# Where the leaves of a streamed weight tree lie in DRAM, and in how many transfers they are sent there

## The chip, the cores and the metric

The kernel runs on one core of one Trainium2 chip. The metric is device time in microseconds (us). Four runs of the kernel before took 1063.92 to 1066.34 us, with a median of 1065.5 us.

## What is computed

The kernel computes an attention block followed by a SwiGLU feed-forward block, all in float32:

```
kv  = einsum('bhsd,bhse->bhde', k, v)              # b 8, h 8, s 576, d 64
out = einsum('bhsd,bhde->bhse', q, kv)
x   = out / sqrt(mean(out*out, -1) + 1e-6) * g_norm  # -> 4608 tokens x 512
g   = x @ w_gate                                   # 512 x 1536
y   = (g * sigmoid(g) * (x @ w_val)) @ w_out       # 1536 x 512
```

## The kernel before

The 4608 tokens are cut into nine blocks of 512. For each block the kernel makes x (attention), then h = silu(x w_gate) * (x w_val) in an "Up" part, then y = h w_out in a "Down" part. The attention work of the next block is laid into these two parts.

**Fewer multiplications by Strassen's scheme.** Block 0 uses plain matrix products. In block 1 the Up part takes one level of a scheme with seven products (numbered 1 to 7) in place of eight. From block 2 on (`DEEP = 2`) the Up part takes two levels, that is 49 products of quarter-size operands; they are executed at L580. Each product needs a linear combination of pieces of w_gate and w_val. Such a combination for outer product o and inner product p is called a leaf (o, p): a [128, 128] tile for each of the two halves f of a pair d. 16 of the 49 leaves lie in the resident weights; the other 33 are made once, in block 1, sent to DRAM, and streamed back in every block from 2 to 8.

**Block 1.** Its Up part has six units, one for each pair j of feature tiles. A unit executes its products in the order 1, 5, then 4 and 3 of the unit before, then 6, 2, 7 (`Up.sequence`). Each product shows as 8 records of TensorE at L431 and takes about 1.73 us. Around them:

- POOL makes three of the operands (t tiles, from a pool of nine buffers) by subtractions at L111, and the products h at L112.
- ACT copies PSUM after product 1 (L447), 6 (L451) and 7 (L482), and takes the SiLU after product 2 (L478) and 4 (L487). All of these accumulate in one PSUM chain b, so product 4 must wait until the copy L482 has read what product 7 left.
- DVE adds (L110) the PSUM chains a and c to tiles r in SBUF, sums parts of h (s and h, `h_sums`), and makes the leaves.

**Making the leaves.** After a product that was the last to use an operand, `multiply` extends a list `making` by the steps of `leaf_steps`: a source is split into quarters, two DVE instructions change one quarter in place, and two more write three further leaves into a room (r for the t tiles, one xi tile for wg and wv, used again by every unit). After each product `make(3)` takes three steps off the list. The last step of each call of `leaf_steps` is `send`, which writes the leaves to DRAM. A pair j thus has 5 + 5 + 5 + 9 = 24 steps.

**Layout in DRAM.** The stream reads leaves in chunks of two, in the order in which the products of blocks 2 to 8 use them (`CHUNKS`, 17 for each d, where d counts two pairs). Before the change every chunk has a DRAM tile of its own, [128, 2, 2, 128] with 2 KB in each partition's row. So a read of a chunk is one contiguous run of 2 KB per partition (L659), and the sends have to pick the leaves of a source apart: two leaves of one source that share a chunk go in one transfer (L711), all others singly (L715). That is 23 transfers for a pair, 138 in all.

**What sets the order.** The instructions of each engine stand in an order that a scheduler makes at build time, by data dependences and program order; the sends among themselves are kept in program order by `tc.keep_in_program_order`. All transfers named here go through the queue of SyncE (SP), which issues them one after the other and waits at each for what it needs: k and v loads (L223), q loads (L238), the sends, the stream loads and the output stores (L814).

**The ring of t tiles.** The nine buffers serve the operands of block 1, then three sets of differences of w_out for the Down part (t<-wo at L111), then the chunks of the stream. A buffer that was sent from is free only when the send has landed.

Of the kernel before, what the change touches and what calls it, by code (L numbers as in the profile page):

```python
# [8 lines left out]
F32 = mybir.dt.float32  # L9
# [5 lines left out]
P = 128  # L15
# [3 lines left out]
def kernel(  # L19
# [41 lines left out]
    nc = tc.nc  # L61
# [11 lines left out]
    NP = NF // 2  # L73
# [5 lines left out]
    def pool(name, bufs, **kw):  # L79
        return ctx.enter_context(tc.tile_pool(name=name, bufs=bufs, **kw))  # L80
# [9 lines left out]
    dram = pool("dram", 1, space=bass.MemoryType.DRAM)  # L90
# [27 lines left out]
    class Words:  # L118
# [12 lines left out]
        def __init__(self, src, shape):  # L131
            self.raw = ld_pool.tile([P, 2 * BLK], U32, name="ld")
            dst = self.raw.rearrange("p (a b) -> p a b", a=shape[0])
            nc.sync.dma_start(out=dst, in_=src)
            self.shape = shape
# [317 lines left out]
    class Up(Quad):  # L453
# [41 lines left out]
        def multiply(self, p):  # L495
            super().multiply(p)
            ffn = self.ffn
            if ffn.n != DEEP - 1:
                return

            if p == 5:
                self.leaf_room = ring().rearrange("p f (s c) -> p (f s) c", c=P)
            if p in (5, 7, 4):
                at = 3 * (5, 7, 4).index(p)
                ffn.making.extend(leaf_steps(self.j, [(self.w[p].unsqueeze(1), (p,))], self.leaf_room[:, at:]))
            if p == 3:
                if ffn.leaf_room is None:
                    ffn.leaf_room = x_pool.tile([P, 3, 7, P], F32, name="xi").rearrange("p a b c -> p (a b) c")
                halves = lambda t: t[self.j].rearrange("p (o i) c -> p o i c", o=2)
                ffn.making.extend(leaf_steps(self.j, [(halves(wg), (1, 2)), (halves(wv), (6, 3))], ffn.leaf_room))  # L510

    class Inner:
# [114 lines left out]
    RESIDENT = (1, 6, 2, 3)  # L627
    QUARTER = {1: (0, 0), 6: (0, 1), 2: (1, 0), 3: (1, 1)}

    CHUNKS = (  # L630
# [5 lines left out]
    class Stream:  # L636


        def __init__(self):
            self.dram = {}  # L640
            for d in range(NP // 2):
                for c in range(len(CHUNKS)):
                    self.dram[d, c] = dram.tile([P, 2, 2, P], F32, name=f"w{d}_{c}")
            self.at = {op: (c, i) for c, ops in enumerate(CHUNKS) for i, op in enumerate(ops)}
            self.tiles, self.uses, self.next, self.held = {}, {}, [], []

        def enable(self, n):
            if DEEP <= n < NB:
                self.next += [(n, d, c) for d in range(NP // 2) for c in range(len(CHUNKS))]
                self.pump()  # L650

        def pump(self):

            while self.next and not self.held[-9]:
                n, d, c = key = self.next.pop(0)
                k = len(CHUNKS[c])
                self.tiles[key] = t_tile(key).rearrange("p l (f c) -> p l f c", f=2)
                self.uses[key] = 2 * k
                nc.sync.dma_start(out=self.tiles[key][:, 0:k], in_=self.dram[d, c][:, 0:k])  # L659

        def use(self, n, d, o, p, f):
            c, i = self.at[o, p]
# [9 lines left out]
    stream = Stream()  # L672

    def t_tile(key=None):

        stream.held.append(key)
        return t_pool.tile([P, 2, 2 * P], F32, name="t")

    def leaf_steps(j, sources, room):


        d, f = divmod(j, 2)
        at = {}
        i = 0
        for t, os in sources:
            n = len(os)
            t = t.rearrange("p o i (e c) -> p o i e c", e=2)
            b11, t2_, b22 = t[:, :, 0, 0], t[:, :, 0, 1], t[:, :, 1, 1]
            to = room[:, i : i + 3 * n].rearrange("p (o r) c -> p o r c", r=3)
            yield lambda b22=b22, t2_=t2_: sub(nc.vector, t2_, b22, t2_)  # L690
            yield lambda b11=b11, t2_=t2_: add(nc.vector, t2_, t2_, b11)
            yield lambda t=t, t2_=t2_, to=to, n=n: sub(
                nc.vector, to[:, :, 0:3:2], t[:, :, 1], t2_.unsqueeze(2).to_broadcast([P, n, 2, P])
            )
            yield lambda b11=b11, t2_=t2_, to=to: sub(nc.vector, to[:, :, 1], b11, t2_)
            for m, o in enumerate(os):
                for r, p in enumerate((4, 7, 5)):
                    at[o, p] = room, i + 3 * m + r
                if o not in RESIDENT:
                    quarters = t[:, m].rearrange("p i e c -> p (i e) c")  # L700
                    for r, p in enumerate((1, 6, 2, 3)):
                        at[o, p] = quarters, r
            i += 3 * n

        def send():
            for c, ops in enumerate(CHUNKS):
                dst = stream.dram[d, c]
                places = [at.get(op) for op in ops]
                if len(ops) == 2 and None not in places and places[0][0] is places[1][0]:
                    (src, i), (_, k) = places  # L710
                    tc.keep_in_program_order(nc.sync.dma_start(out=dst[:, :, f], in_=src[:, i : k + 1 : k - i]))  # L711
                    continue
                for m, place in enumerate(places):
                    if place:
                        tc.keep_in_program_order(nc.sync.dma_start(out=dst[:, m, f], in_=place[0][:, place[1]]))  # L715

        yield send

    class Down(Quad):
        def __init__(self, ffn):  # L720
# [85 lines left out]
    class Ffn:  # L806
# [22 lines left out]
        def up(self, fill):  # L829

            self.s1 = s_pool.tile([P, NP, HB], F32, name="s1")
            units = []
            for d in range(NP // 2):
                if self.n < DEEP:
                    units += [Up(self, 2 * d), Up(self, 2 * d + 1)]
                else:
                    shared = {}
                    units += [Inner(self, d, g, shared) for g in range(4)]
            units[0].prepare()
            last = None  # L840
            for i, this in enumerate(units):
                if i + 1 < len(units):
                    units[i + 1].prepare()
                for unit, p in this.sequence(last):
                    if unit:
                        unit.multiply(p)
                        self.make(3)
                last = this
                fill.get(12 * (i + 1) // len(units), lambda: None)()
            self.down_ = Down(self)  # L850
            self.down_.turn_t(5)
            for unit, p in last.sequence(None):
                if unit is None:
                    last.multiply(p)
# [146 lines left out]
```

## Time and profile before

| | |
|---|---|
| median of 4 runs | 1065.5 us |
| the profiled execution | 1065.41 us, span 1063.6 us |
| PE busy | 1037.6 us, 98% of the span |
| DVE, ACT, POOL busy | 700.7, 245.1, 366.6 us |
| Up part of block 1 | about 162 to 249 us |
| sends to DRAM (w<-t, w<-r, w<-xi) | 138 transfers, 64 or 128 KB each, 1.8 to 2.2 us from issue to landing |
| stream loads (t<-w) | 336 of 256 KB and 21 of 128 KB, median 2.9 and 2.7 us to landing |
| Down part of block 1 | about 249 to 290 us |
| blocks 2 to 6 | about 112 us each |

PE, DVE, ACT, POOL and SP are the engines TensorE, VectorE, ScalarE, GpSimd and SyncE; PEld are TensorE's weight loads. A group "r<-a" is an instruction that writes a tile called r from one called a; L431 is a line of the kernel. In a timeline the columns are start, duration, engine, line, operation, tiles and shapes; a bracket at the end gives the idle time of the engine before it and what ended it. "DMA share" is the mean busy share of 16 DMA engines.

### The profile page before, as it was taken

The numbers are of one execution on the slowest core, as the hardware profiler recorded it, in microseconds if no ns is written. First come the engines' busy times: TensorE is split into PE (matmuls) and PEld (weight loads), VectorE is DVE, ScalarE is ACT, GpSimd is POOL, SyncE is SP. The second block draws the span as 40 slices with busy tenths as digits, with TensorE's granted clock in tenths as the row PEclk, the third lists the DMA queues.
The fourth block names the chain that finished last, engine by engine and source line by source line (L and its number), as shares of the span: only waits on it lengthen the run. The fifth ranks groups of instructions, "written<-read, shape, count | busy, mean of one in ns | idle before, by whom it ended". The sixth has DMA issues, their size and how long they took to land.

```text
span 1063.6 us, 21805 instructions
## 1 busy us (share of the span) xinstructions
PE 1037.6 (98%) x8780; PEld 935.4 (88%) x8780; DVE 700.7 (66%) x1245; ACT 245.1 (23%) x392; POOL 366.6 (34%) x280
## 2 busy tenths in 40 slices
PE   5899999988999999999999999999999999999998
PEld 4644788877899989998999899989999899989997
DVE  2999596778556765576666666666567566765661
ACT  2665111221221211222112211121112221212210
POOL 0000453344025701462156305640456026602670
PEclk8899999998999999999999999999999999999999
DMA  8887103565578326741576246714683265126611
GB/s 236 232 267 224 57 9 107 161 173 160 164 209 251 98 75 193 234 149 61 164 244 170 83 126 229 224 53 129 214 237 77 80 208 190 55 81 189 198 37 40
DMA packets 154644, 161.87 MB, mean 152 GB/s; under 512 B 48432, under 2 KB 105648, under 8 KB 154544
## 3 DMA queue, kind: packets, MB, share of 16 engines
q1 hardware_dynamic: 154480, 160.48, 50.4%
q8 instruction: 70, 1.15, 0.4%
q14 instruction: 30, 0.25, 0.1%
q0 software_dynamic: 64, 0.00, 0.0%
HBM read 138.02 MB, written 22.41 MB: 151 GB/s over the span
## 4 chain that ended last, share of the span: by engine, by line
PE 93%; DVE 3%; SPq 2%; DMA 1%; POOL 1%; issue 0%; ACT 0%; DVEq 0%; POOLq 0%
PE b L580 25%; PE b L431 20%; PE c L580 12%; PE c L431 10%; PE a L580 6%; PE a L431 5%; PE b L882 4%; PE c L882 4%; PE m L255 2%; PE m L339 2%; PE m L292 1%; SPq L223 1%; PE b L292 1%; PE b L272 1%; DMA ld<-in_moe_w_gate_dram 1%; PE m L272 1%
## 5 line engine op out<-in xcount | busy, mean ns | idle before, releaser
L110 POOL TENSOR_TENSOR r<-r 128x256 f32<-128x256 f32 (+1 forms) x105 | 110.2, 1056 | 365.5 <-DVE r L110 361.2
L110 DVE TENSOR_TENSOR r<-b,r 128x512 f32<-128x512 f32 (+1 forms) x273 | 162.3, 607 | 61.3 <-PE b L580 56.5
L110 DVE TENSOR_TENSOR r<-c,r 128x512 f32<-128x512 f32 (+1 forms) x179 | 109.2, 620 | 98.9 <-PE c L580 56.0
L111 POOL TENSOR_TENSOR t<-wo 128x512 f32<-128x512 f32 x81 | 113.2, 1424 | 161.3 <-DVE wo L110 108.5
L580 PE MATMUL b<-x,t 128*128 128x128 f32 x1092 | 151.2, 276 | 0.0
L580 PEld LDWEIGHTS b<-x,t 128*128 128x128 f32 x1092 | 136.0, 192 | 0.6
L110 DVE TENSOR_TENSOR r<-a,r 128x512 f32<-128x512 f32 (+1 forms) x99 | 62.6, 632 | 83.1 <-PE a L580 53.1
L112 POOL TENSOR_TENSOR h<-r 128x1024 f32<-128x1024 f32 (+1 forms) x40 | 81.5, 2053 | 93.2 <-DVE r L110 79.7
L580 PE MATMUL c<-xi,t 128*128 128x128 f32 x840 | 112.1, 275 | 0.0
L580 PEld LDWEIGHTS c<-xi,t 128*128 128x128 f32 x840 | 102.8, 192 | 0.0
L431 PE MATMUL b<-t,h 128*128 128x256 f32 x432 | 97.1, 381 | 0.0
L431 PE MATMUL b<-wo,h 128*128 128x256 f32 x432 | 96.2, 379 | 0.0
L431 PEld LDWEIGHTS b<-wo,h 128*128 128x128 f32 x432 | 81.4, 190 | 10.7
L431 PEld LDWEIGHTS b<-t,h 128*128 128x128 f32 x432 | 80.7, 190 | 11.1 <-issue 0.2
L594 ACT COPY r<-b 128x512 f32<-128x512 f32 x63 | 36.9, 586 | 219.1 <-PE b L580 191.7
L580 PE MATMUL b<-xi,t 128*128 128x128 f32 x588 | 79.7, 276 | 0.0
L580 PEld LDWEIGHTS b<-xi,t 128*128 128x128 f32 x588 | 72.4, 192 | 0.0
L580 PE MATMUL b<-x,wg 128*128 128x128 f32 x336 | 53.0, 280 | 0.0
L580 PE MATMUL b<-x,wv 128*128 128x128 f32 x336 | 51.2, 275 | 0.0
L431 PE MATMUL c<-t,s 128*128 128x256 f32 x216 | 48.9, 383 | 0.0
L431 PE MATMUL a<-wo,h 128*128 128x256 f32 x216 | 48.3, 379 | 0.0
L431 PE MATMUL c<-wo,h 128*128 128x256 f32 x216 | 48.1, 379 | 0.0
(129 smaller groups left out, 1647.2 us busy)
## 6 DMA issues: line engine op xcount, KB each, us to landing
t<-w SPq DMA_DIRECT2D x336, 256.0 KB, 2.9
out_dram<-r SPq DMA_DIRECT2D x17, 512.0 KB, 2.9
ld<-in_q_dram SPq DMA_DIRECT2D x29, 256.0 KB, 4.4
ld<-in_moe_w_gate_dram SPq DMA_DIRECT2D x12, 512.0 KB, 5.1
ld<-in_moe_w_val_dram SPq DMA_DIRECT2D x12, 512.0 KB, 5.2
ld<-in_moe_w_out_dram SPq DMA_DIRECT2D x12, 512.0 KB, 4.3
w<-t SPq DMA_DIRECT2D x36, 128.0 KB, 2.1
ld<-in_k_dram SPq DMA_DIRECT2D x26, 160.0 KB, 3.1
```

Source lines behind the costliest of these rows:

```text
L110: add = lambda e, o, a, b: e.tensor_tensor(out=o, in0=a, in1=b, op=OP.add)
L111: sub = lambda e, o, a, b: e.tensor_tensor(out=o, in0=a, in1=b, op=OP.subtract)
L112: mul = lambda e, o, a, b: e.tensor_tensor(out=o, in0=a, in1=b, op=OP.mult)
L223: nc.sync.dma_start(out=t[r * D : (r + 1) * D, :, 0 : m * D], in_=src[self.n, hs, s0 : s0 + m * D].rearrange("h (p t) d -> p h (t d)", t=m),)
L255: nc.tensor.matmul(self.kv_ps[r][u * D : (u + 1) * D, j, :], lhsT=self.k[j][rows, u, c, :], rhs=self.v[j][rows, u, c, :], start=(c == 0), ...
L272: nc.tensor.transpose(ps[:, j], self.q[t][:, j], ident)
L292: nc.tensor.matmul(self.ps[i][u][p : p + D, t, j, :], lhsT=self.qt[rows, 2 * i + t, j, p : p + D], rhs=kvs[b % 3][rows, j, :], start=True, ...
L339: nc.tensor.transpose(ps[:, e, t], xt[:, t, j + e], ident)
L431: nc.tensor.matmul(banks[e][:, e], lhsT=lhsT, rhs=rhs, start=first and i == 0 and (e == 0 or banks[0] is not banks[1]), stop=i == self.ste ...
L580: nc.tensor.matmul(ps[:, i, f], lhsT=self.weight(o, p, f), rhs=self.operand(o, p), start=first and (i, f) == (0, 0), stop=True, skip_group ...
L594: nc.scalar.copy(out=dst, in_=ps)
L882: nc.tensor.matmul(t, lhsT=w[f // 2][:, i, P * (f % 2) : P * (f % 2 + 1)], rhs=x[:, i, of], start=(i == 0), stop=(i == NS - 1),)
```

## The change

The DRAM tiles of a chunk each give way to one tile for each d, [128, 33, 2, 128], in which the leaves lie in the order in which they are made (`LEAVES`): first the four quarters of each of the sources 5, 7 and 4, then the three further leaves of each source. So four quarters lie side by side, and so do the three (or six) leaves of a room.

`send` now takes one run of leaves. `leaf_steps` yields it as soon as the run is made: for a t source the four quarters after the third step and the three leaves of the room after the fourth; for wg and wv six leaves of xi each. That is 8 transfers for a pair. A pair has 6 + 6 + 6 + 10 = 28 steps, and `up` calls `make(4)` in place of `make(3)`.

A read of a chunk now takes two leaves of the tile with a stride. In 7 of the 17 chunks the two lie side by side (2 KB runs as before), in 9 they don't (two runs of 1 KB), and one chunk has a single leaf.

```
+    LEAVES = [(o, p) for o in (5, 7, 4) for p in (1, 6, 2, 3)]
+    LEAVES += [(o, p) for os in ((5,), (7,), (4,), (1, 2), (6, 3)) for o in os for p in (4, 7, 5)]
...
-            for d in range(NP // 2):
-                for c in range(len(CHUNKS)):
-                    self.dram[d, c] = dram.tile([P, 2, 2, P], F32, name=f"w{d}_{c}")
-            self.at = {op: (c, i) for c, ops in enumerate(CHUNKS) for i, op in enumerate(ops)}
+            self.dram = [dram.tile([P, len(LEAVES), 2, P], F32, name=f"w{d}") for d in range(NP // 2)]
+            self.places = [sorted(map(LEAVES.index, ops)) for ops in CHUNKS]
+            self.at = {LEAVES[i]: (c, m) for c, places in enumerate(self.places) for m, i in enumerate(places)}
...
-                nc.sync.dma_start(out=self.tiles[key][:, 0:k], in_=self.dram[d, c][:, 0:k])
+                nc.sync.dma_start(out=self.tiles[key][:, 0:count], in_=self.dram[d][:, i : k + 1 : max(k - i, 1)])
...
+        def send(leaf, count, src):
+            at = LEAVES.index(leaf)
+            tc.keep_in_program_order(nc.sync.dma_start(out=stream.dram[d][:, at : at + count, f], in_=src))
...
+            if os[0] not in RESIDENT:
+                yield lambda t=t, o=os[0]: send((o, 1), 4, t[:, 0].rearrange("p i e c -> p (i e) c"))
             yield lambda b11=b11, t2_=t2_, to=to: sub(nc.vector, to[:, :, 1], b11, t2_)
-            for m, o in enumerate(os):
-                for r, p in enumerate((4, 7, 5)):
-                    at[o, p] = room, i + 3 * m + r
-                if o not in RESIDENT:
-                    quarters = t[:, m].rearrange("p i e c -> p (i e) c")
-                    for r, p in enumerate((1, 6, 2, 3)):
-                        at[o, p] = quarters, r
+            yield lambda i=i, n=n, o=os[0]: send((o, 4), 3 * n, room[:, i : i + 3 * n])
             i += 3 * n
-
-        def send():
-            for c, ops in enumerate(CHUNKS):
...
-        yield send
...
-                        self.make(3)
+                        self.make(4)
```

More of the change, by code (lines that the diff above doesn't have):

```diff
@@ L639, in __init__ @@
         def __init__(self):
-            self.dram = {}
-            for d in range(NP // 2):
-                for c in range(len(CHUNKS)):
-                    self.dram[d, c] = dram.tile([P, 2, 2, P], F32, name=f"w{d}_{c}")
-            self.at = {op: (c, i) for c, ops in enumerate(CHUNKS) for i, op in enumerate(ops)}
+            self.dram = [dram.tile([P, len(LEAVES), 2, P], F32, name=f"w{d}") for d in range(NP // 2)]
+            self.places = [sorted(map(LEAVES.index, ops)) for ops in CHUNKS]
+            self.at = {LEAVES[i]: (c, m) for c, places in enumerate(self.places) for m, i in enumerate(places)}
             self.tiles, self.uses, self.next, self.held = {}, {}, [], []
@@ L655, in pump @@
                 n, d, c = key = self.next.pop(0)
-                k = len(CHUNKS[c])
+                i, k = self.places[c][0], self.places[c][-1]
+                count = len(CHUNKS[c])
                 self.tiles[key] = t_tile(key).rearrange("p l (f c) -> p l f c", f=2)
-                self.uses[key] = 2 * k
-                nc.sync.dma_start(out=self.tiles[key][:, 0:k], in_=self.dram[d, c][:, 0:k])
+                self.uses[key] = 2 * count
+                nc.sync.dma_start(out=self.tiles[key][:, 0:count], in_=self.dram[d][:, i : k + 1 : max(k - i, 1)])
         def use(self, n, d, o, p, f):
@@ L682, in leaf_steps @@
         d, f = divmod(j, 2)
-        at = {}
         i = 0
+        def send(leaf, count, src):
+            at = LEAVES.index(leaf)
+            tc.keep_in_program_order(nc.sync.dma_start(out=stream.dram[d][:, at : at + count, f], in_=src))
         for t, os in sources:
@@ L694, in leaf_steps @@
             )
+            if os[0] not in RESIDENT:
+                yield lambda t=t, o=os[0]: send((o, 1), 4, t[:, 0].rearrange("p i e c -> p (i e) c"))
             yield lambda b11=b11, t2_=t2_, to=to: sub(nc.vector, to[:, :, 1], b11, t2_)
-            for m, o in enumerate(os):
-                for r, p in enumerate((4, 7, 5)):
-                    at[o, p] = room, i + 3 * m + r
-                if o not in RESIDENT:
-                    quarters = t[:, m].rearrange("p i e c -> p (i e) c")
-                    for r, p in enumerate((1, 6, 2, 3)):
-                        at[o, p] = quarters, r
-            i += 3 * n
-        def send():
-            for c, ops in enumerate(CHUNKS):
[L707 to L715, printed above, removed]
-        yield send
+            yield lambda i=i, n=n, o=os[0]: send((o, 4), 3 * n, room[:, i : i + 3 * n])
+            i += 3 * n
     class Down(Quad):
```

## The prediction

> **What bounds the kernel now.** I read the page first: PE is busy 98% of the span and the chain that ended last is 93% PE. So a change in transfers can only pay where PE stands. The busy times by stretch find that place (columns: stretch, its length, busy PE, weight loads, DVE, ACT, POOL, then granted clock, DMA share, GB/s):
>
> ```profile
> 184.00:200.00 16.00, 16.00 (x107) 13.77 (x99) 14.56 (x34) 4.47 (x8) 3.98 (x4) 1.00 0.55 155
> 215.00:230.00 15.00, 13.51 (x63) 11.56 (x63) 12.48 (x28) 2.77 (x5) 6.25 (x5) 1.00 0.76 182
> 230.00:250.00 20.00, 15.02 (x69) 12.82 (x68) 13.09 (x34) 3.93 (x7) 6.49 (x5) 0.83 0.54 152
> 292.00:404.00 112.00, 112.00 (x1064) 106.42 (x1063) 71.42 (x120) 22.76 (x36) 42.68 (x32) 1.00 0.53 157
> ```
>
> From 117 to 961 us PE is full everywhere but in 200 to 250 us: the Up part of block 1, where the leaves are made. Blocks 2 to 7 show no PE idle at all. PE's own timeline gives the holes:
>
> ```profile
> 228.13 1.99 PE L431 MATMUL b<-x,t 128*128 128x256 f32 x8 [1.49 <-ACT r L482]
> ...
> 242.67 3.75 PE L431 MATMUL b<-x,t 128*128 128x256 f32 x8 [4.98 <-ACT r L482]
> 246.21 2.20 PE L431 MATMUL c<-x,wv 128*128 128x256 f32 x8
> ```
>
> Both are product 4 of a unit, waiting for ACT's copy at L482; the second runs at a reduced clock. [...]L482 stands behind the SiLU L478, which waits for DVE's addition r<-a of after2. The chain of waits through the longest hole says why that addition is late:
>
> ```profile
> 231.93 2.11 DMA w<-t
> ...
> 234.20 1.26 POOL t L111
> 235.46 1.24 POOL h L112
> 236.70 0.02 issue
> 236.72 0.43 DVE s L110
> ```
>
> A send of leaves holds a t buffer; POOL waits for it with a subtraction into that buffer; the product h is queued behind on POOL; DVE's s waits for h, and r<-a is behind s. Read so, the sends are to blame. But the timelines of POOL and DVE show a second limit:
>
> ```profile
> 202.58 1.37 POOL L111 TENSOR_TENSOR t<-wg,wv 128x512 f32<-128x512 f32 x1 [1.63 <-PE b L431]
> ...
> 202.54 0.28 DVE L111 TENSOR_TENSOR t<-t 128x128 f32<-128x128 f32 x1
> 202.86 1.24 DVE L110 TENSOR_TENSOR t<-t 128x128 f32<-128x128 f32 x1
> ```
>
> The same small addition takes 0.29 us when POOL is quiet and 1.24 when it starts inside a POOL instruction: it ends only after POOL does. An addition from PSUM (r<-c at 214.69) keeps its 0.68 beside POOL. So the two engines take turns on all that comes from SBUF. Laying their timelines over each other, I find both idle between 186 and 241 us for only about 1.0 us (0.65 at 205.1, 0.32 at 233.9). When POOL waits for a send, DVE works, and the reverse: the pair itself is nearly full.
>
> [...]
>
> **The change, part by part.** The profiled execution took 1065.41 us (span 1063.6), the median of the runs is 1065.5: no correction.
>
> *Sends.* 138 transfers (36+42+36+18+6 on the page) become 48 of the same bytes. Their start to start on SP is about 0.61 us, so SP's issue falls from 84 to 29 us, an estimate. SP issued from 184 to 275 us almost without pause; that queue disappears. Larger sends land later: 64 KB took 1.8, 128 KB 2.1, 256 KB loads 2.9 us; I take 2.8 for four leaves and 3.5 for six (2.1 to 4 as bounds). They are issued right after the step that makes them, so t and xi buffers come free earlier. On SP the k, v loads of L223 (8 x 0.65) and the q loads of L238 (3.1 us) stay ahead of some sends, as before.
>
> *Steps.* A pair's 24 steps become 28, but make takes 4 in place of 3 for each of 7 products: 28 of 28, where 21 of 24 fell behind. The order of the built programs shows the effect on DVE: the xi subtractions of a unit stand one unit earlier. Before r<-a of unit 2 (counting from 0) there are three more of them, before those of units 4 and 5 four more: 2 x 0.60 + 2 x 0.34 = 1.9 us. Outside block 1 DVE, POOL, ACT and PE keep their order.
>
> *What it is worth at most.* 1.49 + 4.98, 0.28 ahead of the product at 214.29, and the slow clock (3.75 + 1.99 - 2 x 1.73 = 2.28): 9.0 us.
>
> *What the pair lets through.* One unit costs POOL 5 x 1.27 = 6.4 us. DVE from SBUF: three times 1.16 for the t leaves, 1.6 each for wg and wv, 0.34 each for s and h: 7.4. Together 13.8 us against 7 x 1.73 = 12.1 of PE. The last two distances between r<-a agree: 13.84 (212.42 to 226.26) and 14.45 (to 240.71). So with no wait for a send at all, PE still waits. To 240.71 I add the 1.9 us of xi work done earlier and take off the 1.0 us of common idle and 0.8 us for additions from PSUM (three of 0.60 a unit) that POOL can now lie over: between 0 and 1.6, taken at 0.2 a unit for four units. That is +0.1: stalls of 6.85 us in place of 6.75. They move forward: POOL waited 4.61 us for a send until 199.69; now its three subtractions follow h at 195.07 and take turns with DVE ahead of r<-a, which comes near 200.6 instead of 196.12. L478 and L482 (1.2 us) then end near 202, and product 4 due at 200.41 waits 1.5 to 2.5 us. Units 3 to 5 each add about 1.5. [...]the half clock of 2.28 us goes. Sum: 0.1 - 2.3 = -2.2 us, **1063.2**.
>
> *Stream loads.* Nine of 17 chunks become two runs of 1 KB instead of one of 2 KB. They are hidden: SP waits for PE to free a buffer (159 us in all on L659), nine buffers at 51 chunks in 58 us run some 9 us ahead, and a load lands in 2.9 us (longest 6.4). DMA share is 0.81 at 340 to 350[...]. Cost 0; if the cover fails, 0 to 1 us a block.
>
> **Rivals.**
> A, the chain is right: freeing the sends takes all PE waits away. For it: POOL waited 16.5 us for sends in 162 to 250. Against: the 1.0 us of common idle. It gives 1065.4 - 9.0 = 1056.4.
> B, the freed POOL takes the SBUF turn from DVE just ahead of r<-a,[...] so the half clock stays. Stalls 6.75 + 1.9 + 0.3 = 8.9, plus 2.3, against 9.0: +2.2, **1067.6**, slower.[...]
> C, the split loads come late behind the k, v loads in blocks 2 to 8: 7 x 0.7 us eats the gain, 1068. Against: PE never waited there.
> That the change does not do what it says is excluded: the built program has 48 sends.
>
> **How the numbers follow.** A measurement of this kernel tells about 0.2%, 2.1 us, from no change. My case has 0.62, own range 1061.5 to 1064.5; it straddles that bound, so 0.36 faster, 0.24 within, 0.02 slower. A 0.14 (faster), B 0.20 and C 0.04 (slower). Faster 0.50, same 0.24, slower 0.26. The range of 1058.5 to 1068 leaves out most of A and the worse ends of B and C.
>
> **What would show it.** Right: POOL's wait for w<-t is near nothing, yet product 4 waits for L482 in several units, first near 200 us[...]; r<-a is still about 14 us apart; the clock stays 1.00 from 230 to 250; SP has pauses. Wrong: PE full from 184 to 250 (A), one long hole with a clock below 1 (B), PE idle after 292 (C).

## The result and the profile after

The kernel after takes 1063.6 us (median of 41 runs, 1062.06 to 1064.88) beside 1065.1 us of the kernel before (61 runs, 1062.87 to 1066.65). The ratio is 0.9984, with a 95% interval of 0.998 to 0.9989: 1.7 us faster (1.2 to 2.1). So many runs tell it from no change, but it lies inside the 0.2% that the prediction took as the bound. The profiled execution took 1064.45 us, with a span of 1062.6 us (before 1063.6).

The busy times by stretch, kernel after (stretch, length, busy PE, weight loads, DVE, ACT, POOL, granted clock, DMA share, GB/s):

```profile
184.00:200.00 16.00, 16.00 (x92) 13.79 (x83) 15.76 (x30) 2.77 (x5) 7.34 (x6) 1.00 0.81 229
215.00:230.00 15.00, 12.96 (x59) 10.75 (x57) 13.63 (x30) 3.94 (x8) 5.73 (x4) 1.00 0.97 236
230.00:250.00 20.00, 17.80 (x81) 15.31 (x82) 17.19 (x42) 4.76 (x9) 5.37 (x4) 0.91 0.53 154
292.00:404.00 112.00, 112.00 (x1065) 106.45 (x1064) 71.33 (x120) 22.81 (x36) 42.66 (x32) 1.00 0.54 158
```

Blocks 2 to 7 are as full as before. The difference lies where the prediction put it, in 200 to 250 us. PE's own timeline there:

```profile
201.75 1.99 PE L431 MATMUL b<-x,t 128*128 128x256 f32 x8 [1.67 <-ACT r L482]
...
216.49 1.99 PE L431 MATMUL b<-x,t 128*128 128x256 f32 x8 [0.88 <-ACT r L482]
...
230.26 1.99 PE L431 MATMUL b<-x,t 128*128 128x256 f32 x8 [1.42 <-ACT r L482]
...
241.76 2.87 PE L431 MATMUL b<-x,t 128*128 128x256 f32 x8 [1.94 <-ACT r L482]
244.42 2.72 PE L431 MATMUL c<-x,wv 128*128 128x256 f32 x8
246.97 0.38 PE L272 MATMUL b<-ident,ld 128*128 128x128 f32 x2
```

In place of two waits of product 4 (1.49 and 4.98 us) there are four short ones, 5.91 us in all beside 6.47. But the last eight records still stretch to 2.87, and the next eight to 2.72: from start to start that is 2.66 and 2.55 us beside 1.73, so 1.75 us are still lost to a slow clock (granted 0.91 in 230 to 250 us, before 0.83). Read in the same way, the kernel before lost 2.12 us: its records start at 242.67, 246.21 and 248.25. The waits are 0.56 us shorter and the slow clock costs 0.37 us less, together 0.9 of the 1.0 us between the two spans.

POOL's timeline of the kernel after shows the moved work:

```profile
194.69 3.12 POOL L111 TENSOR_TENSOR t<-wg,wv 128x512 f32<-128x512 f32 x2
197.76 1.44 POOL L111 TENSOR_TENSOR t<-wv 128x512 f32<-128x512 f32 x1
```

The three subtractions follow h at 193.34 at once, with no wait for a send. They take turns with DVE, whose r<-a of unit 2 comes at 199.87 instead of 196.12. The same instruction of DVE ahead of it takes 0.42 us in the kernel before, where POOL stood, and 1.48 us in the kernel after. First before, then after:

```profile
195.79 0.42 DVE L111 TENSOR_TENSOR wg<-wg 128x256 f32<-128x256 f32 x1
196.12 0.68 DVE L110 TENSOR_TENSOR r<-a,r 128x512 f32<-128x512 f32 x1
```

```profile
198.01 1.48 DVE L111 TENSOR_TENSOR wg<-wg 128x256 f32<-128x256 f32 x1
...
199.87 0.68 DVE L110 TENSOR_TENSOR r<-a,r 128x512 f32<-128x512 f32 x1
```

### The profile page after: what moved, and what is told of

It reads as the page before. It is cut to its first block, busy times and chain, and to the rows that moved or that the text cites. A ratio compares the mean times of both kernels' runs of the same rounds, so it can differ in the third digit from the quotient of the medians.

```text
span 1062.6 us, 21679 instructions
## 1 busy us (share of the span) xinstructions
PE 1037.3 (98%) x8780; PEld 935.2 (88%) x8780; DVE 708.7 (67%) x1245; ACT 244.9 (23%) x392; POOL 369.2 (35%) x280
## 4 chain that ended last, share of the span: by engine, by line
PE 93%; DVE 3%; DMA 1%; SPq 1%; issue 1%; POOL 0%; ACT 0%; DVEq 0%; ACTq 0%; POOLq 0%
PE b L580 25%; PE b L431 20%; PE c L580 12%; PE c L431 10%; PE a L580 6%; PE a L431 5%; PE b L870 4%; PE c L870 4%; PE m L255 2%; PE m L339 2%; PE m L292 1%; SPq L223 1%; PE b L292 1%; PE b L272 1%; DVE xi L111 1%; DMA ld<-in_moe_w_gate_dram 1%
## 5 line engine op out<-in xcount | busy, mean ns | idle before, releaser
L594 ACT COPY r<-b 128x512 f32<-128x512 f32 x63 | 36.9, 586 | 219.1 <-PE b L580 191.7
L111 DVE TENSOR_TENSOR h<-h 128x1536 f32<-128x1536 f32 x18 | 35.2, 1957 | 19.6 <-PE b L431 19.6
```

The source lines that it names most:

```text
L111: sub = lambda e, o, a, b: e.tensor_tensor(out=o, in0=a, in1=b, op=OP.subtract)
L594: nc.scalar.copy(out=dst, in_=ps)
```

## The experiments

The ratios are to runs of the kernel before on the same chip. "Stalls" are the PE waits that the timeline shows in 190 to 292 us of the profiled execution, "clock" is the lowest granted clock of a stretch there. Both are read from one execution, while the median is that of several: the profiled execution of kernel 8 took 2.0 us more than the median, that of kernel 2 1.4 and that of the kernel after 0.8 more, that of kernel 6 1.6 less.

| kernel | median us | ratio to before (95%) | stalls us | clock |
|---|---|---|---|---|
| before | 1065.1 | | 6.47 | 0.83 |
| after | 1063.6 | 0.998 to 0.9989 | 5.91 | 0.91 |
| 1 pace alone | 1067.8 | 1.0018 to 1.0036 | 8.69 | 0.89 |
| 2 layout alone | 1061.1 | 0.9947 to 0.9974 | 5.13 | 0.91 |
| 3 t on DVE | 1060.1 | 0.9938 to 0.9963 | 3.26 | 1.00 |
| 4 leaves in Down | 1060.1 | 0.9935 to 0.996 | 3.06 | 1.00 |
| 5 both reliefs | 1056.9 | 0.9901 to 0.9928 | 0.62 | 1.00 |
| 6 before, leaves in Down | 1063.0 | 0.9954 to 0.9979 | 3.83 | 1.00 |
| 7 sends twice | 1093.7 | 1.0241 to 1.0269 | | 0.84 |
| 8 more leaves in Down | 1060.5 | 0.9936 to 0.9961 | 4.26 | 0.95 |
| 9 after, 23 sends | 1062.5 | 0.9958 to 0.998 | 5.32 | 1.00 |
| 10 both reliefs, 23 sends | 1056.6 | 0.9902 to 0.9929 | 0.71 | 1.00 |
| 11 both reliefs, make(3) | 1057.4 | 0.9908 to 0.9935 | 0.94 | 1.00 |
| 12 after, 8 late sends | 1062.9 | 0.9968 to 0.9988 | 5.74 | 1.00 |

### The two halves of the change

**1, the pace alone.**

```
 (kernel before)
-                        self.make(3)
+                        self.make(4)
```

> The kernel before (chunk layout, 23 sends for a pair) with make(4) in place of make(3); nothing else. Three theories for the 1.5 us between before (1065.1) and after (1063.6). Sends: fewer and earlier sends are the gain, so the pace alone gives nothing, 1065.1 (1064.6 to 1065.6), POOL still waits some 16 us for w<-t in 162 to 250 us. Pace: the steps made one unit earlier are the gain, so 1063.6. Pair (POOL and DVE take turns on SBUF, and their sum per unit exceeds PE's): no work is taken away, so the stalls of PE stay near 6 to 7 us; [...]anything between 1063 and 1066, with both engines idle together under 1.5 us between 186 and 241 us.

It is slower than before by 0.27%, outside all three ranges. DVE's timeline of this kernel shows a wait that neither before nor after has:

```profile
208.16 0.43 DVE L111 TENSOR_TENSOR xi<-wg 128x256 f32<-128x256 f32 x1 [5.04 <-DMA w<-xi]
...
216.14 0.68 DVE L110 TENSOR_TENSOR r<-a,r 128x512 f32<-128x512 f32 x1
```

The subtraction into xi now stands ahead of r<-a, and waits 5.04 us until the send of the unit before has left xi. POOL stands too: laid over each other, the timelines of both show 5.5 us of common idle between 186 and 241 us. PE then has its longest hole, 4.34 us, in front of the product at 218.01. Why the send is so late, the timeline of SP's queue says (start, length, line, what is issued):

```profile
208.86 0.52 SPq L711 DMA_DIRECT2D w<-t  x1
...
223.30 3.06 SPq L238 DMA_DIRECT2D ld<-in_q_dram  x4
```

Between these two lies the issue of one pair's 23 sends, almost without a pause: 14.4 us, 0.63 us a send. A unit has 12.1 us of PE. The kernel before is alike: its last full pair takes SP 13.6 us (228.11 to 241.70). The waits of its SP queue in 186 to 250 us come to 9.7 us, none of them over 0.8, beside 36.9 us in the kernel after. The three largest groups of the kernel before (waiting for; us in total, times, longest):

```profile
SPq L711 <- DVE r L111: 2.2, 5, 0.8
SPq L715 <- DVE t L111: 1.3, 4, 0.5
SPq L715 <- DVE r L111: 1.0, 2, 0.5
```

**2, the layout alone.**

```
 (kernel after)
-                        self.make(4)
+                        self.make(3)
```

> The kernel after (leaves in order of making, 8 sends for a pair) with make(3) in place of make(4): 126 of 168 steps are called in Up, the rest spill into Down. Sends: same as after, 1063.6 (1063.1 to 1064.1). Pace: back to 1065.1. Pair: about 32 more steps, some 10 us of DVE time, leave the Up part for the Down part, where DVE is busy only about 60% of the time, so the stalls of PE shrink and the time falls to 1059 to 1062; unless t buffers, whose leaves are now made late, come free too late, which would show as POOL waiting over 10 us for DVE or for w<-t.

It is faster than the kernel after by about 2.5 us (0.9961 against 0.9984), as the pair theory had it, though the profiled execution waits hardly less (5.13 us in place of 5.91): the waits at units 3 and 4 are gone, but the last grows to 3.31 us. r<-a of units 3 to 5 comes 1.6 to 3.1 us earlier than after (at 213.06, 225.25 and 238.02). Ahead of unit 4 two xi subtractions fewer stand; ahead of unit 3 they are as many, but POOL's subtraction t<-wo, which the kernel after starts there at 211.58, comes only at 221.76. The pace costs about the same in both layouts, 2.5 to 2.9 us.

**12, eight sends, issued late.**

```
             if os[0] not in RESIDENT:
-                yield lambda t=t, o=os[0]: send((o, 1), 4, t[:, 0].rearrange("p i e c -> p (i e) c"))
+                sends.append(((os[0], 1), 4, t[:, 0].rearrange("p i e c -> p (i e) c")))
...
-            yield lambda i=i, n=n, o=os[0]: send((o, 4), 3 * n, room[:, i : i + 3 * n])
+            sends.append(((os[0], 4), 3 * n, room[:, i : i + 3 * n]))
             i += 3 * n
+        yield lambda: [send(*s) for s in sends]
```

> The kernel after, same layout and 8 sends for a pair, but the sends of a source (or of wg and wv together) are issued in one last step, as before the change: 24 steps for a pair, make(4). DVE's order of instructions is the same as in the kernel after. With the pace alone (1067.8; same steps, 23 sends) it differs in layout and number of transfers, with the kernel after (1063.6) only in when the sends are issued. Queue full: the 23 old sends took 14.4 us of SP a unit and so were a bound of their own, 8 sends take some 4 us and are none, early or late, so 1063.6 within 1. Time of issue: the early send of the four quarters and of wg's six leaves is what freed the buffers, so 1065.5 to 1067.8, with POOL or DVE waiting for w<-t or w<-xi just ahead of r<-a.

1062.9 us, and the interval overlaps that of the kernel after. But the edit did not make the sends late: in the trace they stand in the same order, and up to 240 us each is issued within 0.9 us of its time in the kernel after (a pair's two sends of xi at 195.28 and 198.40, there at 194.72 and 198.12). So what late sends would cost isn't shown. Beside the pace alone, which takes the same 24 steps at make(4), it is 5.0 us faster. Layout, number and order of the transfers differ and, by the scheduler's choice, the places of some xi subtractions among their neighbours on DVE and of some of POOL's instructions. So at this pace the new layout gains 5 us, and SP's queue no longer fills up (its six sends from 201.43 to 209.37 us take 0.36 us each, with pauses between). That the second is the cause of the first is not shown by this run.

**9, 23 sends in the new layout.**

```
+            for i, k in {4: ((0, 2), (2, 2)), 3: ((0, 1), (1, 1), (2, 1)), 6: ((0, 2), (2, 2), (4, 1), (5, 1))}[count]:
+                dst = stream.dram[d][:, at + i : at + i + k, f]
+                tc.keep_in_program_order(nc.sync.dma_start(out=dst, in_=src[:, i : i + k]))
```

> The kernel after, layout, steps and make(4) as they are, but each send is cut into the sizes that the sends before had: four leaves into 2 + 2, three into 1 + 1 + 1, six into 2 + 2 + 1 + 1, so 23 transfers for a pair again, with no byte more and no wait between them. It tells whether the 4.2 us between the pace alone (1067.8) and the kernel after (1063.6) come from the number of transfers on SP's queue. Count: 138 issues of 0.5 to 0.6 us fill SP's queue from 184 us on again, so 1067 to 1068.5, with SP without pauses and POOL and DVE idle together for some 5 us. Pair as the only cause: the number of transfers does not count, 1063.6 to 1064.2, and the 4.2 us belong to something else in the layout.

The number of transfers alone is not it: 1062.5 us, 1.1 us below even the range of the pair theory, and no idle time common to POOL and DVE of over 0.1 us in 186 to 241 us. The SP queue of this kernel:

```profile
222.00 1.59 SPq L691 DMA_DIRECT2D w<-t  x2
...
234.20 0.88 SPq L691 DMA_DIRECT2D w<-t  x2
```

Here 23 sends take 12.2 us, 0.53 us each, which just keeps up with PE. Three things differ from the pace alone: each send is issued a little faster, the sends come in the order of making (wg's six ahead of wv's), and the scheduler put some xi subtractions up to four places earlier on DVE. At the wait of 5.04 us the order of DVE is not what differs: the subtraction into xi stands behind the same instructions as there, but runs at 205.01 without a wait, since its sends begin at 201.75 in place of 203.68 and those of wg come first. Which of the three saves the 5 us as a whole stays open. What it shows is that 23 sends, issued right after the steps that make them, do no harm in the new layout.

**7, each send twice.**

```
-            tc.keep_in_program_order(nc.sync.dma_start(out=stream.dram[d][:, at : at + count, f], in_=src))
+            for _ in range(2):
+                tc.keep_in_program_order(nc.sync.dma_start(out=stream.dram[d][:, at : at + count, f], in_=src))
```

> The kernel after with each of the 48 sends issued twice, one behind the other (96 transfers, twice the bytes; nothing else). Pair: t and xi buffers come free some 1 to 3 us later, but POOL and DVE are busy with other work meanwhile: 1063.6 to 1064.6. Sends: what was gained by going from 138 to 48 is lost again for 96, so 1065 to 1067. If only the number of transfers counts (SP's issue, 0.4 to 0.6 us each), 96 lie in the middle between 48 and 138.

30 us slower than after, far outside every range, because it does more than double the number. The waits of SP's queue in this kernel, 162 to 330 us:

```profile
SPq L690 <- DMA w<-t: 20.9, 15, 2.8
SPq L690 <- DMA w<-r: 19.7, 15, 2.9
SPq L690 <- DMA w<-xi: 16.3, 10, 3.2
```

The second send writes the same place as the first, so SP waits until that has landed, 57 us in all, with everything behind it. It says nothing on the number of transfers; kernel 9 was run in its place.

### The pair of POOL and DVE

**3, the t subtractions on DVE.**

```
 (kernel after)
-                sub(nc.gpsimd, t[-1], b, t2)
+                sub(nc.vector, t[-1], b, t2)
```

> The kernel after with the three subtractions of Up.prepare on DVE in place of POOL. Pair: three POOL instructions of 1.27 us become three DVE ones of about 0.60, so the sum of the two engines falls from 13.8 to about 11.8 us a unit, below PE's 12.1: the distance between r<-a falls to about 12.1 to 12.5, PE's stalls in 200 to 250 us fall from 5.9 to under 2, no slow clock, 1056 to 1059. Sends: the wait for w<-t moves from POOL to DVE, where r<-a is queued behind it, so stalls stay or grow, 1063.6 to 1066. DVE alone (its own sum with the additions from PSUM would be 7.4 + 1.8 + 1.8 = 11.0 of 12.1): not a bound yet.

**4, leaves in Down.**

```
 (kernel after)
-                ffn.making.extend(leaf_steps(self.j, [(halves(wg), (1, 2)), (halves(wv), (6, 3))], ffn.leaf_room))
+                late = ffn.later if self.j >= 2 else ffn.making
+                late.extend(leaf_steps(self.j, [(halves(wg), (1, 2)), (halves(wv), (6, 3))], ffn.leaf_room))
...
                 self.make(12)
+                self.making = self.later[0:8]
+                del self.later[0:8]
+                self.make(8)
```

> The kernel after, where the ten steps on wg and wv of pairs 2 to 5 are put on a second list that is worked off in the Down part, eight steps after each product. The t leaves stay in Up at the same pace. Pair: 30 steps that were in Up, some 9.7 us of DVE time, leave it, 3.2 us for each of units 3 to 5, so the pair needs about 10.6 us a unit there: the stalls from 210 us on go, and the clock stays full, 1057 to 1060; PE stays full in Down, as DVE is busy about 60% of it. Sends: the sends of t leaves are as before, so 1063.6 within 0.5. A rival on the other side: the leaves or their sends come late in Down and PE, DVE or the stream waits there, 1064 to 1067, with PE idle after 250 us.

Both come to 1060.1 us, 3.5 us faster than after. That is 1.1 us short of the pair theory's range for the first and at the slow end of it for the second, and far from the 1063.6 of the sends theory. PE's timelines, first of kernel 3, then of kernel 4:

```profile
228.17 1.99 PE L431 MATMUL b<-x,t 128*128 128x256 f32 x8 [1.42 <-ACT r L482]
239.57 1.99 PE L431 MATMUL b<-x,t 128*128 128x256 f32 x8 [1.84 <-ACT r L482]
```

```profile
202.37 1.99 PE L431 MATMUL b<-x,t 128*128 128x256 f32 x8 [1.67 <-ACT r L482]
217.10 1.99 PE L431 MATMUL b<-x,t 128*128 128x256 f32 x8 [0.87 <-ACT r L482]
239.26 1.96 PE L431 MATMUL b<-x,t 128*128 128x256 f32 x8 [0.52 <-ACT r L482]
```

In kernel 3 DVE has more to do than after, and PE waits less. So it isn't DVE's work alone that held PE, but that POOL's instructions shut DVE out (1.48 us in place of 0.42 for the subtraction shown above). The relief is smaller than worked out: r<-a comes 13.2, 14.9, 13.8 and 11.4 us apart, and only the first of these is shorter than in the kernel after (14.5). The last of the moved subtractions ends at 209.5 us, so the last two distances hold none; why the second did not shrink stays open. DVE is busy for 50.8 of the 55 us from 186 to 241, in the kernel after for 52.8, with the time in which POOL shuts it out counted as busy. In kernel 4 the waits at units 4 and 5 nearly vanish, where its work was taken away, and those of units 2 and 3 stay, where none was. Layout and number of the sends are those of the kernel after in both; in kernel 4 the sends of xi of pairs 2 to 5 move to Down with their steps.

**5, both reliefs.** The edits of 3 and 4 together:

```
-                sub(nc.gpsimd, t[-1], b, t2)
+                sub(nc.vector, t[-1], b, t2)
...
+                late = ffn.later if self.j >= 2 else ffn.making
```

> The kernel after with both reliefs together: the three subtractions of Up.prepare on DVE, and the ten steps on wg and wv of pairs 2 to 5 worked off in the Down part. Each alone left 3.1 to 3.3 us of PE stalls (201 to 240 us), in different units: the first at units 4 and 5, the second at units 2 and 3. Pair: together none is left over 0.5 us, so another 2.5 to 3.3 us go: 1056.8 to 1057.6. DVE alone: it now carries 12.2 us a unit in units 0 to 2 and waits for sends itself, so stalls of 1 to 3 us come back, 1058 to 1061. Sends: no more than either alone, 1060.

```profile
213.63 2.00 PE L431 MATMUL b<-x,t 128*128 128x256 f32 x8 [0.28 <-ACT r L482]
235.76 2.00 PE L431 MATMUL b<-x,t 128*128 128x256 f32 x8 [0.34 <-ACT r L482]
```

1056.9 us, as the pair theory had it: 0.9914 of before, and the ceiling that the prediction worked out (1056.4) all but reached. Of PE's waits 0.62 us are left.

**6, the leaves in Down with the old sends.** The edit of 4 in the kernel before:

```
 (kernel before)
+                late = ffn.later if self.j >= 2 else ffn.making
```

> The kernel before (chunk layout, 23 sends for a pair, make(3)) with the steps on wg and wv of pairs 2 to 5 worked off in the Down part, eight after each product, as in the run with the leaves in Down. It tells what the old sends cost once the pair is relieved. Pair as the only cause: the stalls of units 3 to 5 go as they did with the new sends, 1065.1 less about 5, 1059.5 to 1061. Pair and sends both (the pace alone made both engines idle together for 5.5 us, which the old sends must have caused): the queue of SP keeps t buffers, so 1061.5 to 1063.5, with POOL and DVE idle together for over 1.5 us in 186 to 241. Sends as the only cause: no gain, 1065.

1063.0 us is in the range of "pair and sends both": 2.9 us more than kernel 4, which has the new sends and make(4). But the sign given with it did not show: POOL and DVE are never idle together for over 0.1 us in 186 to 241 us. So here the way in which the old sends cost time is not shown. Its five runs fall apart as well, two at 1061.4 us and three from 1063.0 to 1063.7, and the trace is of one of the two.

**10, both reliefs and 23 sends.** The edits of 5 and 9 together:

```
 (kernel 5)
+            for i, k in {4: ((0, 2), (2, 2)), 3: ((0, 1), (1, 1), (2, 1)), 6: ((0, 2), (2, 2), (4, 1), (5, 1))}[count]:
```

> The kernel with both reliefs (1056.9), its sends cut into 23 for a pair in the same way. Count and pair independent of each other: the 23 sends cost about as much as without relief, 3 to 5 us, so 1060 to 1062. Pair first: once POOL and DVE have time to spare, a late buffer finds slack, and the sends cost under 1.5 us, 1057 to 1058.4. With t on DVE a wait for a send would hold r<-a directly, which speaks for the first.

1056.6 us: with time to spare on POOL and DVE, 23 sends cost nothing that can be measured (1056.9 with eight).

**8, more leaves in Down.**

```
 (kernel 4)
-                late = ffn.later if self.j >= 2 else ffn.making
+                late = ffn.later if self.j >= 1 else ffn.making
...
-                self.make(8)
+                self.make(10)
```

> The kernel with the leaves in Down, with pair 1 moved as well (50 steps, ten after each of five products of Down). Pair: the stall of 0.87 us at unit 3's product 4 goes, that at unit 2's (1.67 us) shrinks only by what of pair 1's steps stood ahead of it; 1058 to 1059.5. DVE in Down: it has about 14 us free of 42, and now gets about 13 us; if that is too much, PE stands after 250 us and the time is 1060 to 1062.

1060.5 us. The wait at unit 3 goes as expected, but PE's timeline has a new one in Down:

```profile
274.37 1.75 PE L339 MATMUL m<-ident,r 128*128 128x128 f32 x8 [2.14 <-DVE r L112]
```

DVE is late there with the next block's attention. The 0.9 us won in Up is lost in Down: 2.14 us of waiting, and a slow clock after it in this execution, the slowest of five (granted 0.83 in 270 to 280 us; the next 24 records took 6.38 us, where three products of 1.73 are 5.19).

**11, both reliefs at make(3).**

```
 (kernel 5)
-                        self.make(4)
+                        self.make(3)
...
-                self.making = self.later[0:8]
+                self.making += self.later[0:8]
```

> The kernel with both reliefs and make(3) in place of make(4): the 18 steps of the t sources of a pair fit into 21 places, so fewer steps stand in a row ahead of r<-a. Pair: the kernel with both reliefs has 0.6 us of PE stalls left between 201 and 241 us, so at most 0.6 us are to be had: 1056.3 to 1056.9. Late buffers: t buffers come free up to one product (1.7 us) later, 1057 to 1058.

1057.4 us, and 0.94 us of waits: nothing more was to be had. The time lies in the late-buffer range, but its interval overlaps that of kernel 5, so late buffers are not shown.

## Why the prediction was right, and where not

**The place and the net.** Forecast 1063.2, measured 1063.6; -2.2 us forecast, -1.7 measured. That the net came so close is in part luck: it was to be all clock, with waits 0.1 us longer, and in the profiled execution it was 0.56 us of waits and 0.37 of clock. Of the signs that were named, POOL's small wait for sends (2.1 us from 186 us on), the waits of product 4 in several units (0.88 to 1.94 us) and the pauses of SP came; the clock of 1.00 from 230 to 250 us did not (0.91). The stream loads cost nothing, as said: 112.00 of 112.00 us, though a load lands in 3.1 instead of 2.9 us. That POOL and DVE hold each other up carried the forecast rightly. In 160 to 250 us of the traces of before and after, DVE starts 35 instructions on tiles in SBUF inside one of POOL's, and 33 of them end 0.15 to 0.55 us after POOL's does; two that read PSUM there (r<-c at 214.69 before, r<-m at 248.25 after) keep their 0.68 us. And kernel 3 moves 3 x 1.27 us of POOL work a unit onto the busier engine and wins 3.5 us.

**Sends.** Landing was taken at 2.8 and 3.5 us; it is 2.9 for 256 KB and 3.4 for 384 KB.

**The pace** was put at +1.9 us. Kernels 1 and 2 give +2.5 to +2.9. The mechanism, more xi work ahead of r<-a, shows in the new layout at unit 4; at unit 3 it is an earlier subtraction of POOL. With the old sends there is a second one that the prediction had not: that xi work waits for a send.

**The layout** was put at -1.0 - 0.8 - 2.3 = -4.1 us. Kernel 2 gives about -4.2 (2.8 to 5.6) and kernel 12 against kernel 1 -5.0. The size was right, the reason only in part. The step that failed is "the pair itself is nearly full", taken as the end of the search. The prediction had 0.61 us a send and 23 sends for a pair, that is 14.0 us a unit, and never set it beside the pair's 13.8: SP's queue was a third limit of about the same size. The trace of kernel 1 shows it at work (14.4 us a pair, and DVE waiting 5.04 us for a send); kernel 9, with 23 sends in 12.2 us, shows that the number of sends alone does not make it one. At the old pace its share can't be separated from that of the DVE steps which kernel 2 moves out of Up.

**Stalls** were put at 6.85 us and measure 5.91. The mis-sized term is the last unit: the 14.45 us up to the last r<-a was read as the pair's need. After, the four distances are 14.5, 14.75, 13.8 and 11.4 us; in the last unit it was a late send that had set it (POOL waited 6.61 us for one until 231.70). The first hole came as worked out: r<-a at 199.87 (200.6 forecast), a wait of 1.67 us (1.5 to 2.5), and the longest was 1.94.

**The slow clock** was to go entirely (-2.28) and in the profiled execution went from 2.12 to 1.75 us. (The 2.28 counts a record's duration of 3.75 us; from start to start it is 3.54.) That it would go was the author's estimate from the length of the waits: before, the eight records after 4.98 us took 3.75 us, those after 1.49 us their usual 1.99. The traces don't bear it out: in the kernel after, those after 1.94 us took 2.87. Kernel 12 has the same wait of 1.94 us at the same product, and its timeline goes on at full speed:

```profile
241.86 1.97 PE L431 MATMUL b<-x,t 128*128 128x256 f32 x8 [1.94 <-ACT r L482]
243.66 1.89 PE L431 MATMUL c<-x,wv 128*128 128x256 f32 x8
```

Its span is 1061.0 us, 1.6 less than that of the kernel after: nearly the whole slow clock. So such a hole was followed by 1.75 us of slow clock in one execution and by none in another; what decides is not shown. Some of the 2.8 us over which the runs of the kernel after spread may be that; only one of them was traced.

**Rivals.** A (the sends are all of it) falls: with pauses in SP's queue PE still waits, and the other 6.7 us came from relieving the pair (kernel 5). B's long hole did not come, but in the profiled execution its slow clock did (0.91). C did not come (112.00 of 112.00 us, as above); its 0.7 us a block was the author's estimate, which no trace of before shows.

## What to carry to other kernels

Before one limit is called the bound, work out the time per period of every serial resource, the queue that issues transfers among them, and set them side by side: here PE had 12.1 us, POOL and DVE together 13.8, and SP's queue 14.0 by the prediction's price (13.6 and 14.4 in two traces). Freeing one of two nearly equal limits brings little (1.7 us here); moving work to a stage where the limiting engines have time brought four times that (6.7 us more), until that stage filled up in its turn. And take the two halves of a change apart: this one was a gain of 4 to 5 us and a loss of 2.5 to 2.9.

## What was not expected of the hardware

After waits of one length the clock was now slow and now not. The eight records of product 4 after each of its waits of over 1.9 us (190 to 292 us, in the order of the waits):

| kernel | wait us | eight records us |
|---|---|---|
| after | 1.94 | 2.87 |
| 12 | 1.94 | 1.97 |
| 9 | 2.12 | 1.96 |
| 7 | 2.93 | 1.99 |
| 1 | 3.04 | 3.44 |
| 2 | 3.31 | 2.79 |
| 1 | 4.34 | 3.34 |
| 7 | 4.63 | 3.75 |
| before | 4.98 | 3.75 |

Those of kernels 12, 9 and (after 2.93 us) 7 took their usual time, the others were slow, and so was kernel 8 after its 2.14 us in Down. So the length of the wait does not tell the two apart here: 1.94 us was followed by both, and 2.93 us by full speed.

How low the clock was and for how long, the table by stretch shows. In the kernel after it was still 1.00 in the stretch that holds the wait, where PE was busy for 1.47 of 3.41 us, and 0.50 in the 3.41 us behind it:

```profile
239.26:242.67 3.41, 1.47 (x10) 1.19 (x8) 3.38 (x9) 1.10 (x2) 0.00 (x0) 1.00 0.40 115
242.67:246.08 3.41, 3.41 (x9) 2.70 (x9) 2.09 (x7) 0.60 (x1) 0.74 (x1) 0.50 0.02 5
```

In the kernel before it was 0.50 for 6.83 us, from 240.01 to 246.84, which begins in the wait of 4.98 us. In kernel 12 it was 1.00 from 230 to 250 us. So a wait of some 2 us was followed by 1.75 us of slow clock or by none; these traces do not show by what.

A send costs SP's queue 0.36 us where the queue is free (kernel after, w<-t at 201.14), and 0.5 to 0.6 us from start to start where sends follow each other (0.53 in kernel 9, 0.63 in kernel 1).
